# Moving the key and value weights, folding the query weights early, copying the first u spectrum on ScalarE, and re-routing the u loads in a fused attention and state-space kernel

## Chip, cores, metric

One core of one Trainium2 chip. The metric is device microseconds (us) of the whole kernel. Times quoted are medians; comparisons use ratios, explained with the result. A single core's run has no second die to compare with, so a run counts as slow only when it is over 1.5% above the fastest of the same kernel, and only fast runs are compared.

## The reference, cut to what matters

Two independent computations whose outputs are concatenated:

```python
# A: linear attention, x is 2048 x 448, 16 heads of 28
q, k, v = split(x @ wqkv)
pq, pk = q @ w_phi, k @ w_phi                       # per head
phi = concat([softmax(p), softmax(-p)])             # for pq and pk
kv, z = sum_s phi_k * v,  sum_s phi_k
a = (phi_q @ kv) / (phi_q @ z + 1e-6) @ wo
# B: state-space convolution, u is 2048 x 448, 256 states per channel
K[d, l] = real(sum_n C[d,n] * exp(dt[d] * A[d,n] * l) * dt[d] * B[d,n])
b = irfft(rfft(pad(u)) * rfft(pad(K))) + u * Dskip
```

## The kernel before

The kernel computes K as products of "low" tables W (49 small positions, by exponentials, sines and multiplies) and "high" tables U, multiplied on TensorE (`build_k`). It does the FFT as matmuls with a table G1; each half of u gives one "signal spectrum". The attention has a "key side" (16 tiles of x, accumulating KV) and a "query side". The weights w_phi are folded into the query and key weights (`fold_weights`) before use. All SBUF memory is one tile cut by hand at byte offsets; the framework finds the overlaps and sets the waits, and it chooses each engine's instruction order when it compiles, by rank and by its own estimate of time. At run time each engine follows that order: below, VectorE's state tables stand 4.16 us behind a sum of u that waits for its load.

The parts that the change touches:

```python
# memory (bytes per partition): W occupies oW .. oW+43904
Wqkv = sb("Wqkv", [112, 4, 3 * D_MODEL], BF16, oW)
wT = sb("wT", ..., oW + 10752); BD = sb("BD", ..., oW + 17920)
WpK = sb("WpK", [112, 4, D_MODEL], BF16, oW + 18816)      # folded key weights
# ... cut ...
def signal_spectrum(b, copy):
    ab = sb("ab", [128, 2, 4, D_MODEL], BF16, oVR)          # sums and differences of u
    for t in range(4):
        ua = sb("ua", [128, 2, D_MODEL], BF16, 0, bufs=2)   # two buffers, shared with the key side's EK
        for a in range(2):
            nc.gpsimd.dma_start(out=ua[64 * a:64 * a + 64, 0, :], in_=rep_rows(u2, 1024 * b, a, t))
        nc.gpsimd.dma_start(out=ua[:, 1, :], in_=pair_rows(u2, 1024 * b, t, 0))
        TT(out=ab[:, 0, t, :], in0=ua[:, 0, :], in1=ua[:, 1, :], op=ALU.add)
        TT(out=ab[:, 1, t, :], in0=ua[:, 0, :], in1=ua[:, 1, :], op=ALU.subtract)
    # ... cut: 8 x (two groups of 4 matmuls, each copied from PSUM by copy(); one store to SUd)
# ... cut: state tables, squarings, transposes of x ...
fold_weights(1, nc.vector.tensor_copy)                      # key weights
for _ in signal_spectrum(0, nc.vector.tensor_copy):         # first u spectrum
    pass

def key_side():                                             # 16 tiles
    for tt in range(16):
        pkv = ps_t.tile([128, 2, 512], F32, name="pkv", tag="arg", bufs=2)   # the tables' arguments use tag "arg" too
        # 4 matmuls with WpK, 4 with the value columns of Wqkv
        # ScalarE: two exponentials and a copy; VectorE: sums, reciprocal, multiply; TensorE: 8 accumulations
# ... cut ...
rotations(0)
with rank(9000):
    key_side()
with rank(8000):
    fold_weights(0, nc.scalar.copy)                         # query weights, after the key side
with rank(10000):
    for c in range(2):
        hi_tables(0, c)
more = signal_spectrum(1, nc.scalar.copy)                   # second u spectrum, interleaved with query_side
# for each quarter qt: dampings (low-table exponentials, ScalarE), damp (multiplies, VectorE), build_k
```

The softmax here doesn't subtract the row's maximum and nothing guards it: scores larger than these inputs give would overflow.

Of the kernel before, what the change touches and what calls it, by code (L numbers as in the profile page):

```python
# [10 lines left out]
BF16 = mybir.dt.bfloat16  # L11
# [6 lines left out]
D_MODEL = 448  # L18
# [70 lines left out]
def rep_rows(x2, row, a, t):  # L89
    rs = x2.ap[0][0]  # L90
    return bass.AP(tensor=x2.tensor, offset=x2[row + 256 * t + 128 * (1 - a), 0].offset,
                   ap=[[2 * rs, 64], [1, D_MODEL]])

def pair_rows(x2, row, t, col):
    rs = x2.ap[0][0]
    return bass.AP(tensor=x2.tensor, offset=x2[row + 1023 - 128 - 256 * t, col].offset,
                   ap=[[128 * rs, 2], [-2 * rs, 64], [1, D_MODEL]])
# [23 lines left out]
def kernel(  # L121
# [17 lines left out]
    nc = tc.nc  # L139
    out2 = out[0]  # L140
    x2 = A_x[0]
    u2 = B_u[0]
    TT = nc.vector.tensor_tensor
    act = nc.scalar.activation
    mm = nc.tensor.matmul
    consts = _dft_tables()
    G_d, GI_d, F_d, P_d, M_d = (nc.inline_tensor(t, name=f"const{i}").ap() for i, t in enumerate(consts))
# [4 lines left out]
    sb = Bytes(sb_pool.tile([128, 212800 // 2], BF16, name="sbuf"))  # L152
# [3 lines left out]
    oPID, oDSK, oMISC, oCB, oAT, oTH, oPW = 5376, 7424, 8320, 8960, 12544, 16128, 19712  # L156
    oW, oU, oT, oT2, oTs, oF, oSK0, oL = 44800, 88704, 117376, 138880, 146048, 151536, 158704, 173040
    PID = sb("PID", [128, 8, 128], BF16, oPID)
# [9 lines left out]
    xT = sb("xT", [112, 4, 2048], BF16, oF)  # L168
# [4 lines left out]
    KVZ = sb("KVZ", [112, 2, 4, 4, 2], BF16, o1 + 1792)  # L173
    HM = sb("HM", [112, 4, D_HEAD + 1], BF16, o1 + 1920)
    oSC, oRZ, oON, oOT, oOF, oVR, oZK, oV = (o1 + x for x in (2152, 3176, 4712, 8296, 10344, 12136, 15848, 16232))
    Wqkv = sb("Wqkv", [112, 4, 3 * D_MODEL], BF16, oW)
    wT = sb("wT", [112, 2, 4, D_MODEL], BF16, oW + 10752)
    BD = sb("BD", [112, 4, 112], BF16, oW + 17920)
    WpK = sb("WpK", [112, 4, D_MODEL], BF16, oW + 18816)

    ldt = sb("ldt", [112, 4], BF16, oMISC + 32)
    raw = {nm: sb(f"raw{nm}", [112, 4, SSM_N], BF16, oT + 2048 * i)
# [13 lines left out]
    for i in range(4):  # L196
        t = sb(f"xs{i}", [128, 4, D_MODEL], BF16, oW + 22400 + 3584 * i)
        nc.sync.dma_start(out=t[:, :, :], in_=x2[512 * i:512 * i + 512, :].rearrange("(t p) d -> p t d", p=128))
        XS.append(t)
    G1 = sb("G1", [128, 2, 4, 512], BF16, oG1)  # L200
    nc.sync.dma_start(out=G1[:, :, :, :], in_=G_d)
    nc.sync.dma_start(out=Wqkv[:, :, :], in_=A_wqkv.rearrange("(j p) n -> p j n", p=112))
    nc.gpsimd.memset(BD[:, :, :], 0.0)
    for hh in range(4):
        nc.gpsimd.dma_start(out=BD[28 * hh:28 * hh + 28, :, 28 * hh:28 * hh + 28],
                            in_=A_w_phi.rearrange("(c h) d f -> h d c f", h=4)[hh])
# [8 lines left out]
        return t.rearrange("p (g q x) -> p q g x", g=4, q=4)  # L215

    def signal_spectrum(b, copy):
        ab = sb("ab", [128, 2, 4, D_MODEL], BF16, oVR)
        for t in range(4):
            ua = sb("ua", [128, 2, D_MODEL], BF16, 0, bufs=2)  # L220
            for a in range(2):
                nc.gpsimd.dma_start(out=ua[64 * a:64 * a + 64, 0, :], in_=rep_rows(u2, 1024 * b, a, t))
            nc.gpsimd.dma_start(out=ua[:, 1, :], in_=pair_rows(u2, 1024 * b, t, 0))
            TT(out=ab[:, 0, t, :], in0=ua[:, 0, :], in1=ua[:, 1, :], op=ALU.add)  # L224
            TT(out=ab[:, 1, t, :], in0=ua[:, 0, :], in1=ua[:, 1, :], op=ALU.subtract)
        i = 0
        for st in range(2):
            for cp in range(2):
                for mp in range(2):
                    sg = sgs[i % 2]  # L230
                    i += 1
                    for k2 in range(2):
                        mt = 2 * mp + k2
                        p = mmt([128, 512])
                        for jt in range(4):
                            mm(p[:, 0:D_MODEL].rearrange("p (q g x) -> p q g x", q=4, g=4),  # L236
                               lhsT=G1[:, cp, jt, 128 * mt:128 * mt + 128], rhs=by_quarter(ab[:, cp ^ st, jt, :]),
                               start=(jt == 0), stop=(jt == 3))
                        copy(sg[:, k2, :], p[:, 0:D_MODEL])  # L239
                        if k2 == 0:  # L240
                            yield
                    nc.sync.dma_start(out=SUd[:, b, cp, st, 2 * mp:2 * mp + 2, :], in_=sg[:, :, :])
                    yield
# [58 lines left out]
    for half in range(2):  # L302
        hc, p = state_args(AT, half)
# [3 lines left out]
    for k in LOWP:  # L307
        for half in range(2):
            hc, p = state_args(TH, half)
# [22 lines left out]
    for tt in range(16):  # L332
        p = ps_t.tile([112, 4, 128], BF16, name="xp", tag="kb", bufs=2)
# [4 lines left out]
    def fold_weights(which, copy):  # L338
        for c in range(4):
            p = ps_t.tile([112, D_MODEL], BF16, name="wp", tag="kb", bufs=2)  # L340
            c0 = which * D_MODEL + 112 * c
            for j in range(4):
                nc.tensor.transpose(p[:, 112 * j:112 * j + 112], Wqkv[:, j, c0:c0 + 112], PID[0:112, 0, 0:112])
            copy(wT[:, which, c, :], p[:, :])
        for j in range(4):
            p = ps_t.tile([112, D_MODEL], F32, name="wp", tag="kb", bufs=2)
            for c in range(4):
                mm(p[:, 112 * c:112 * c + 112], lhsT=wT[:, which, c, 112 * j:112 * j + 112], rhs=BD[:, c, :],
                   start=True, stop=True)
            copy((WpQ, WpK)[which][:, j, :], p[:, :])  # L350

    fold_weights(1, nc.vector.tensor_copy)
    for _ in signal_spectrum(0, nc.vector.tensor_copy):
        pass
    V_ = [sb("V", [128, D_HEAD + 1, 16], BF16, oV, bufs=2) for _ in range(2)]
    for v in V_:
# [102 lines left out]
    def key_side():  # L459
        acc = [ps_t.tile([128, 512], F32, name="acc", tag="kb", bufs=2) for _ in range(2)]  # L460
        for tt in range(16):
            ts = slice(128 * tt, 128 * tt + 128)
            pkv = ps_t.tile([128, 2, 512], F32, name="pkv", tag="arg", bufs=2)
            for dj in range(4):
                mm(pkv[:, 0, 0:D_MODEL], lhsT=xT[:, dj, ts], rhs=WpK[:, dj, :], start=(dj == 0), stop=(dj == 3))
            for dj in range(4):
                mm(pkv[:, 1, 0:D_MODEL], lhsT=xT[:, dj, ts], rhs=Wqkv[:, dj, 2 * D_MODEL:], start=(dj == 0),
                   stop=(dj == 3))
            EK = sb("EK", [128, 2, D_MODEL], BF16, 0, bufs=2)
            for s in range(2):  # L470
                act(EK[:, s, :], pkv[:, 0, 0:D_MODEL], ACT.Exp, scale=1.0 - 2.0 * s)  # L471
            V = V_[tt % 2]
            nc.scalar.copy(V[:, 0:D_HEAD, :], pkv[:, 1, 0:D_MODEL].rearrange("p (h d) -> p d h", d=D_HEAD))
            zk = sb("zk", [128, 2, 16], F32, oZK, bufs=2)
            nc.vector.tensor_reduce(zk[:, :, :], EK[:, :, :].rearrange("p s (h f) -> p s h f", f=D_HEAD), axis=AX.X,  # L475
                                    op=ALU.add)
            rk = sb("rk", [128, 2, 16], BF16, oZK + 256, bufs=2)
            with nc.allow_low_precision(reason="bf16 softmax weights, as in the reference"):
                nc.vector.reciprocal(rk[:, :, :], zk[:, :, :])
            VR = sb("VR", [128, 2, D_HEAD + 1, 16], BF16, oVR, bufs=2)  # L480
            TT(out=VR[:, :, :, :], in0=V[:, :, :].unsqueeze(1).to_broadcast([128, 2, D_HEAD + 1, 16]),
               in1=rk[:, :, :].unsqueeze(2).to_broadcast([128, 2, D_HEAD + 1, 16]), op=ALU.mult)
            for s in range(2):
                for c in range(4):
                    mm(acc[s][0:112, 116 * c:116 * c + 116].rearrange("p (d h) -> p d h", h=4),  # L485
                       lhsT=EK[:, s, 112 * c:112 * c + 112], rhs=VR[:, s, :, 4 * c:4 * c + 4],
                       start=(tt == 0 and c == 0), stop=(tt == 15), skip_group_check=True)
        for s in range(2):
            a4 = acc[s][0:112, 0:464].rearrange("p (c d h) -> p c h d", c=4, h=4)
            TT(out=KVN[:, s], in0=a4[:, :, :, 0:D_HEAD],  # L490
               in1=HM[:, :, 0:D_HEAD].unsqueeze(1).to_broadcast([112, 4, 4, D_HEAD]), op=ALU.mult)
            TT(out=KVZ[:, s, :, :, 0], in0=a4[:, :, :, D_HEAD],
               in1=HM[:, :, 0].unsqueeze(1).to_broadcast([112, 4, 4]), op=ALU.mult)
            nc.vector.tensor_copy(KVZ[:, s, :, :, 1], HM[:, :, 0].unsqueeze(1).to_broadcast([112, 4, 4]))
# [183 lines left out]
    @contextmanager  # L678
    def rank(p):
        old = tc.cur_priority  # L680
        tc.cur_priority = p
        yield
        tc.cur_priority = old
# [4 lines left out]
    rotations(0)  # L688
    with rank(9000):
        key_side()  # L690
    with rank(8000):
        fold_weights(0, nc.scalar.copy)
    with rank(10000):
        for c in range(2):
            hi_tables(0, c)
# [89 lines left out]
```

## Time and profile before

| reading of the profiled run | before |
|---|---|
| median time (3 runs) | 390.0 us |
| VectorE / TensorE / ScalarE busy | 310.9 / 282.2 / 219.1 us |
| key side's last operation on VectorE ends | 114.5 us |
| first low-table exponential | 115.9 us |
| fourth tile of u's second half summed from | 128.1 us |
| large low-table multiplies start | 139.4 us |
| first build matmul | 157.0 us |
| activation table loads | 17 |

The table of windows, in four stretches: up to 50 us, to the end of the key side, to the first build matmul, to the end of the span. Columns: stretch, its length, then busy time and instruction count of each engine, the granted TensorE clock, the DMA share and GB/s.

```profile
core 0: us, PE busy (x) PEld busy (x) DVE busy (x) ACT busy (x) POOL busy (x), PEclk, DMA share, GB/s
0.00:50.00 50.00, 20.70 (x138) 14.47 (x139) 33.42 (x40) 32.21 (x50) 11.19 (x23) 0.88 0.64 159
50.00:114.50 64.50, 54.04 (x382) 32.48 (x381) 60.44 (x127) 28.43 (x59) 4.58 (x11) 0.96 0.11 35
114.50:157.00 42.50, 28.56 (x184) 16.30 (x184) 22.42 (x49) 24.36 (x45) 5.43 (x9) 0.72 0.16 47
157.00:390.00 233.00, 178.93 (x3078) 140.93 (x3076) 194.65 (x335) 134.09 (x230) 12.93 (x17) 0.85 0.29 83
```

In the second stretch VectorE is the fullest (60.4 of 64.5 us). In the third no engine is full: that is the hole.

What ScalarE does at the edge of the hole, from its timeline (start, duration, engine, line, operation, operands, and in brackets the idle time before it and what ended it). L471 and L473 are the key side, L344 a copy of the query fold, L407 a low-table exponential:

```profile
109.91 0.54 ACT L473 CAST sbuf<-pkv 128x448 bf16<-128x448 f32 x1
114.41 1.58 ACT L344 COPY sbuf<-wp 112x448 bf16<-112x448 bf16 x3 [3.96 <-PE wp L343]
115.88 0.93 ACT L407 ACTIVATE sbuf<-arg 128x896 bf16<-128x896 f32 x1
116.69 0.55 ACT L344 COPY sbuf<-wp 112x448 bf16<-112x448 bf16 x1
```

ScalarE stands idle for 4 us, then the fold goes first. Further on, in ScalarE's queue a query exponential (L504) waits for the query projection on TensorE (L501):

```profile
120.39 1.01 ACT L407 ACTIVATE sbuf<-arg 128x896 bf16<-128x896 f32 x1
127.61 1.08 ACT L504 ACTIVATE sbuf<-mmt 112x512 bf16<-112x512 f32 x2 [6.21 <-PE mmt L501]
128.58 0.55 ACT L407 ACTIVATE sbuf<-arg 128x448 bf16<-128x448 f32 x1
```

That projection in turn stands in TensorE's queue behind the second spectrum (L236), which waits for the third tile of u:

```profile
126.62 0.53 PE L236 MATMUL mmt<-sbuf 128*128 128x448 bf16 x1 [4.59 <-DVE sbuf L224]
```

TensorE had finished the tables' arguments by 111.4 us, and the fold was over at 120.6. On VectorE inside the hole (L224 is a sum of u, L419 a low-table multiply):

```profile
118.77 0.39 DVE L224 TENSOR_TENSOR sbuf<-sbuf 128x448 bf16<-128x448 bf16 x1 [4.25 <-DMA sbuf<-in_B_u_dram]
...
126.17 0.39 DVE L224 TENSOR_TENSOR sbuf<-sbuf 128x448 bf16<-128x448 bf16 x1 [4.86 <-DMA sbuf<-in_B_u_dram]
...
128.09 0.39 DVE L224 TENSOR_TENSOR sbuf<-sbuf 128x448 bf16<-128x448 bf16 x1
...
135.75 0.60 DVE L419 TENSOR_TENSOR sbuf<-sbuf 128x112 bf16<-128x112 bf16 x4 [6.97 <-ACT sbuf L404]
...
139.40 0.97 DVE L419 TENSOR_TENSOR sbuf<-sbuf 128x1680 bf16<-128x1680 bf16 x1
```

And the start of VectorE's timeline (L336 copies a transposed tile of x; L254 is the first state-table multiply, which everything else in the state tables follows):

```profile
10.43 0.42 DVE L336 COPY sbuf<-xp 112x512 bf16<-112x512 bf16 x1 [9.57 <-PE xp L335]
15.02 0.39 DVE L224 TENSOR_TENSOR sbuf<-sbuf 128x448 bf16<-128x448 bf16 x1 [4.16 <-DMA sbuf<-in_B_u_dram]
15.33 0.16 DVE L247 TENSOR_SCALAR sbuf<-sbuf 112x4 bf16<-112x4 bf16 x1
15.40 2.36 DVE L254 TENSOR_TENSOR sbuf<-sbuf 112x1024 f32<-112x1024 bf16 x2
```

VectorE's queue stands 4.16 us at the first sum of u, for a load, with the state tables behind it.

### The profile page before, as it was taken

Reading aid. Unit: us, or ns where it says so; the run is one execution under the profiler, and the core shown is the slowest. Engines: PE = TensorE matmul, PEld = TensorE weight load, DVE = VectorE, ACT = ScalarE, POOL = GpSimd, SP = SyncE. Lnnn points to the kernel's source line nnn. Section 1 sums busy time; section 2 is a strip of 40 time slices with the busy share of each in tenths; the row PEclk is TensorE's granted clock in tenths of the full one; section 3 lists DMA queues with packets and bytes.
Section 4 is the critical chain, followed back from the end, with each engine's and each line's share of the span. In section 5 each row is a group of like instructions: output and inputs, shape, how many; then the busy total and the mean of one; then the engine's idle time right before and its main releaser. Section 6 shows DMA issues by size and latency. Waiting matters only on the chain.

```text
span 389.2 us, 9018 instructions
## 1 busy us (share of the span) xinstructions
PE 282.2 (73%) x3780; PEld 204.2 (52%) x3780; DVE 310.9 (80%) x548; ACT 219.1 (56%) x381; POOL 34.1 (9%) x59
## 2 busy tenths in 40 slices
PE   0294478988863859996787799677970596956994
PEld 0261353455452335674554576445860485945994
DVE  0598988999961279996459988998996979999872
ACT  1289972055554764799985846942949323212431
POOL 7100220000033000000000000001000000054000
PEclk9999569999995687999659699885986888796999
DMA  7990212200012001213000100120922218397005
GB/s 184 284 254 28 63 28 72 94 24 2 0 30 64 28 25 45 70 56 96 26 24 25 25 28 26 24 79 24 278 97 56 52 52 290 104 205 180 14 3 189
DMA packets 31105, 31.60 MB, mean 81 GB/s; under 512 B 11560, under 2 KB 28680, under 8 KB 30680
## 3 DMA queue, kind: packets, MB, share of 16 engines
q1 hardware_dynamic: 24216, 22.65, 20.1%
q0 software_dynamic: 4064, 7.23, 7.2%
q10 hardware_dynamic: 2784, 1.15, 1.3%
q8 instruction: 29, 0.48, 0.5%
q14 instruction: 12, 0.10, 0.1%
HBM read 23.07 MB, written 7.34 MB: 78 GB/s over the span
## 4 chain that ended last, share of the span: by engine, by line
PE 37%; DVE 20%; ACT 17%; DMA 11%; issue 7%; SPq 4%; POOL 3%; DVEq 0%; POOLq 0%; ACTq 0%
PE kb L453 10%; PE mmt L593 6%; DMA sbuf<-in_B_u_dram 5%; PE mmt L545 4%; PE mmt L236 3%; PE yo L634 3%; SPq L567 3%; ACT sbuf L504 3%; DVE sbuf L475 3%; DMA sbuf<-SUd 3%; PE mmt L501 3%; PE arg L373 2%; PE mmt L539 2%; DMA sbuf<-const 2%; DVE sbuf L239 2%
## 5 line engine op out<-in xcount | busy, mean ns | idle before, releaser
L453 PE MATMUL kb<-sbuf 128*16 128x49 bf16 x1792 | 49.3, 274 | 3.7 <-issue 2.9
L593 PE MATMUL mmt<-sbuf 128*128 128x112 bf16 (+1 forms) x336 | 34.4, 272 | 22.2 <-ACT sbuf L596 9.7
L419 DVE TENSOR_TENSOR sbuf<-sbuf 128x112 bf16<-128x112 bf16 (+1 forms) x64 | 37.4, 619 | 13.2 <-ACT sbuf L404 12.8
L453 PEld LDWEIGHTS <-sbuf 128*16 128x16 bf16 x1792 | 41.5, 118 | 9.4 <-issue 7.8
L236 PE MATMUL mmt<-sbuf 128*128 128x448 bf16 x128 | 34.0, 390 | 14.2 <-DVE sbuf L224 6.5
L593 PEld LDWEIGHTS <-sbuf 128*128 128x128 bf16 x336 | 28.6, 118 | 28.5 <-issue 11.2
L425 DVE TENSOR_TENSOR sbuf<-sbuf 128x896 bf16<-128x896 bf16 (+1 forms) x48 | 35.6, 775 | 0.2
L596 ACT CAST sbuf<-mmt 128x448 bf16<-128x448 f32 x32 | 16.2, 549 | 27.1 <-PE mmt L593 27.1
L634 PE MATMUL yo<-sbuf 128*128 128x112 bf16 (+1 forms) x384 | 28.8, 228 | 2.9 <-DMA sbuf<-const 1.8
L471 ACT ACTIVATE sbuf<-pkv 128x448 bf16<-128x448 f32 x32 | 15.8, 552 | 26.5 <-PE acc L485 19.1
L532 DVE TENSOR_TENSOR sbuf<-mmt,sbuf 128x448 bf16<-128x448 f32 x32 | 19.4, 622 | 11.0 <-PE mmt L529 10.7
L634 PEld LDWEIGHTS <-sbuf 128*128 128x128 bf16 x384 | 26.1, 98 | 3.5 <-DMA sbuf<-const 2.0
L610 DVE TENSOR_TENSOR sbuf<-sbuf 128x1792 bf16<-128x1792 bf16 (+1 forms) x18 | 24.4, 1400 | 3.5 <-ACT sbuf L596 3.3
L407 ACT ACTIVATE sbuf<-arg 128x896 bf16<-128x896 f32 (+1 forms) x32 | 25.8, 874 | 1.4 <-PE kb L453 1.4
L236 PEld LDWEIGHTS <-sbuf 128*128 128x128 bf16 x128 | 13.1, 106 | 19.9 <-issue 11.5
L641 ACT CAST sbuf<-yo 128x224 bf16<-128x224 f32 (+1 forms) x24 | 9.0, 410 | 25.2 <-PE yo L636 25.2
L373 PE MATMUL arg<-sbuf 128*128 128x224 bf16 x128 | 22.0, 320 | 1.3 <-ACT sbuf L404 0.7
L504 ACT ACTIVATE sbuf<-mmt 112x512 bf16<-112x512 f32 x32 | 17.2, 601 | 9.8 <-PE mmt L501 9.6
L545 PE MATMUL mmt<-sbuf 112*128 112x448 bf16 x64 | 19.6, 436 | 3.6 <-ACT sbuf L541 3.5
L501 PE MATMUL mmt<-sbuf 112*112 112x512 bf16 x64 | 19.4, 426 | 1.9 <-ACT sbuf L504 1.9
L286 DVE TENSOR_TENSOR sbuf<-sbuf 128x1792 bf16<-128x1792 bf16 (+3 forms) x33 | 20.1, 609 | 0.7
L287 DVE TENSOR_TENSOR sbuf<-sbuf 128x1792 bf16<-128x1792 bf16 (+3 forms) x33 | 19.8, 603 | 0.0
(117 smaller groups left out, 590.5 us busy)
## 6 DMA issues: line engine op xcount, KB each, us to landing
sbuf<-const SPq DMA_DIRECT2D x32, 224.0 KB
SUd<-sbuf SPq DMA_DIRECT2D x16, 224.0 KB
sbuf<-const SPq DMA_DIRECT2D x2, 1024.0 KB
sbuf<-in_A_x_dram SPq DMA_DIRECT2D x4, 448.0 KB
out_dram<-sbuf SPq DMA_DIRECT2D x16, 112.0 KB
sbuf<-SUd POOLq DMA_DIRECT2D x1, 1792.0 KB, 12.6
sbuf<-in_B_u_dram SPq DMA_DIRECT2D x4, 448.0 KB
sbuf<-SUd POOLq DMA_DIRECT2D x2, 896.0 KB, 9.2
```

The costliest lines, as they stand in the source:

```text
L236: mm(p[:, 0:D_MODEL].rearrange("p (q g x) -> p q g x", q=4, g=4), lhsT=G1[:, cp, jt, 128 * mt:128 * mt + 128], rhs=by_quarter(ab[:, cp ^ s ...
L373: mm(p[:, e // 2, (e % 2) * QC:(e % 2 + 1) * QC], lhsT=PID[:, 4 * grp + e, :], rhs=src[:, part, cols], start=(part == 0), stop=(part == 1))
L407: act(dst.rearrange("p c (a b) x -> p a b c x", b=2), src.rearrange("p a b (c x) -> p a b c x", c=2), ACT.Exp, scale=float(sgn * f))
L419: TT(out=W[:, c, cs_, r, :], in0=W[:, c, cs_ if sgn < 0 else 0, r, :], in1=T[:, cs_, j0:j0 + n, xs], op=ALU.mult)
L425: TT(out=(t2[:, :, 0:n, :], dst)[1 - i], in0=src, in1=PW[512][:, i, cols].unsqueeze(1).unsqueeze(1).to_broadcast([128, 2, n, COLS]), op=AL ...
L453: mm(p[32 * g:32 * g + N_HI, qq * N_LO:(qq + 1) * N_LO], lhsT=U[qt % 2][c][:, :, ri, xc], rhs=W[:, c, ri, :, xc], start=(i == 0), stop=(i ...
L501: mm(p[:, :], lhsT=WpQ[:, dj, 112 * c:112 * c + 112], rhs=xT[:, dj, 512 * sc:512 * sc + 512], start=(dj == 0), stop=(dj == 3))
L504: act(EQ[:, s, c, :], p[:, :], ACT.Exp, scale=1.0 - 2.0 * s)
L545: mm(pf[:, :], lhsT=oT_[:, c, :], rhs=wo[:, c, :], start=(c == 0), stop=(c == 3))
L593: mm(p[:, k2, :].rearrange("p (q g x) -> p q g x", q=nq, g=4), lhsT=f_tiles[i][1][:, fi, :], rhs=natural(Kt[:, kt, :], gi), start=(n == 0) ...
L610: TT(out=t[:, :, :], in0=su, in1=sk, op=ALU.mult)
L634: mm(p[:, k2, :], lhsT=GI[r][:, cp, mt, 128 * jt:128 * jt + 128], rhs=S[:, r, cp, mt, :], start=(cp == 0 and mt == 0), stop=False)
```

## The change

Its intent: let the low tables start before the key side is done, by moving the key and value weights out of W's memory and folding the query weights early; relieve VectorE of the first spectrum's copies; bring u by the sync queue.

```diff
-    Wqkv = sb("Wqkv", [112, 4, 3 * D_MODEL], BF16, oW)
-    wT = sb("wT", [112, 2, 4, D_MODEL], BF16, oW + 10752)
-    BD = sb("BD", [112, 4, 112], BF16, oW + 17920)
-    WpK = sb("WpK", [112, 4, D_MODEL], BF16, oW + 18816)
+    Wqk = sb("Wqk", [112, 4, 2 * D_MODEL], BF16, oW)
+    wT = sb("wT", [112, 2, 4, D_MODEL], BF16, oW + 7168)
+    BD = sb("BD", [112, 4, 112], BF16, oW + 14336)
+    WpK = sb("WpK", [112, 4, D_MODEL], BF16, oPW + 17920)
+    WV = sb("WV", [112, 4, D_MODEL], BF16, oPW + 21504)
     # ... cut: Wqk and WV loaded right after x, the G1 load moved behind the folds
     def signal_spectrum(b, copy):
-        ab = sb("ab", [128, 2, 4, D_MODEL], BF16, oVR)
+        ab = sb("ab", [128, 2, 4, D_MODEL], BF16, oT + 14336)
         for t in range(4):
-            ua = sb("ua", [128, 2, D_MODEL], BF16, 0, bufs=2)
+            ua = sb(f"ua{b}", [128, 2, D_MODEL], BF16, (oON, 0)[b], bufs=(4, 2)[b])
     # ... cut: the three loads into ua by nc.sync instead of nc.gpsimd
     fold_weights(1, nc.vector.tensor_copy)
-    for _ in signal_spectrum(0, nc.vector.tensor_copy):
+    fold_weights(0, nc.scalar.copy)
+    nc.sync.dma_start(out=G1[:, :, :, :], in_=G_d)
+    for _ in signal_spectrum(0, nc.scalar.copy):
         pass
     # ... cut: the value matmuls read WV
     with rank(9000):
         key_side()
-    with rank(8000):
-        fold_weights(0, nc.scalar.copy)
```

More of the change, by code (lines that the diff above doesn't have):

```diff
@@ L199 @@
         XS.append(t)
+    wq3 = A_wqkv.rearrange("(j p) n -> p j n", p=112)
+    nc.sync.dma_start(out=Wqk[:, :, :], in_=wq3[:, :, 0:2 * D_MODEL])
+    nc.sync.dma_start(out=WV[:, :, :], in_=wq3[:, :, 2 * D_MODEL:])
     G1 = sb("G1", [128, 2, 4, 512], BF16, oG1)
-    nc.sync.dma_start(out=G1[:, :, :, :], in_=G_d)
-    nc.sync.dma_start(out=Wqkv[:, :, :], in_=A_wqkv.rearrange("(j p) n -> p j n", p=112))
     nc.gpsimd.memset(BD[:, :, :], 0.0)
@@ L217, in signal_spectrum @@
     def signal_spectrum(b, copy):
-        ab = sb("ab", [128, 2, 4, D_MODEL], BF16, oVR)
+        ab = sb("ab", [128, 2, 4, D_MODEL], BF16, oT + 14336)
         for t in range(4):
-            ua = sb("ua", [128, 2, D_MODEL], BF16, 0, bufs=2)
+            ua = sb(f"ua{b}", [128, 2, D_MODEL], BF16, (oON, 0)[b], bufs=(4, 2)[b])
             for a in range(2):
-                nc.gpsimd.dma_start(out=ua[64 * a:64 * a + 64, 0, :], in_=rep_rows(u2, 1024 * b, a, t))
-            nc.gpsimd.dma_start(out=ua[:, 1, :], in_=pair_rows(u2, 1024 * b, t, 0))
+                nc.sync.dma_start(out=ua[64 * a:64 * a + 64, 0, :], in_=rep_rows(u2, 1024 * b, a, t))
+            nc.sync.dma_start(out=ua[:, 1, :], in_=pair_rows(u2, 1024 * b, t, 0))
             TT(out=ab[:, 0, t, :], in0=ua[:, 0, :], in1=ua[:, 1, :], op=ALU.add)
@@ L342, in fold_weights @@
             for j in range(4):
-                nc.tensor.transpose(p[:, 112 * j:112 * j + 112], Wqkv[:, j, c0:c0 + 112], PID[0:112, 0, 0:112])
+                nc.tensor.transpose(p[:, 112 * j:112 * j + 112], Wqk[:, j, c0:c0 + 112], PID[0:112, 0, 0:112])
             copy(wT[:, which, c, :], p[:, :])
@@ L466, in key_side @@
             for dj in range(4):
-                mm(pkv[:, 1, 0:D_MODEL], lhsT=xT[:, dj, ts], rhs=Wqkv[:, dj, 2 * D_MODEL:], start=(dj == 0),
+                mm(pkv[:, 1, 0:D_MODEL], lhsT=xT[:, dj, ts], rhs=WV[:, dj, :], start=(dj == 0),
                    stop=(dj == 3))
```

## The prediction

> **What bounds it now.** VectorE is fullest (the page's busy times): 310.9 us of 389.2; TensorE 282.2, ScalarE 219.1. The table of windows shows three stretches:
>
> - 20 to 114 us: VectorE 84 to 100% busy; in 77 to 114 it has 35.4 of 37 us. TensorE is not far behind (30.4).
> - 114 to 139 us: a hole. VectorE works 5.3 of 25 us, TensorE 16.7 at a granted clock of 0.66, ScalarE 16.8. By the timeline the key side ends at 114.4 us; then the query weights are folded (to 120.6), the first low-table exponential runs at 115.9, the second half of u lands by GpSimd at 118.8, 120.6, 126.2 and 128.1, and the query projection waits on TensorE behind the second spectrum (4.6 us for the third u tile). The large low-table multiplies start only at 139.4.
> - After 139 us: no such hole except 190 to 207 (VectorE 8.5 of 17 us); 160 to 190 is ScalarE's (29.5 of 30).
>
> **What the change does.**
>
> 1. The 16 copies of the first u spectrum (9.25 us of VectorE, windows of that line) go to ScalarE, which has 2.9 of 17 us busy in 60 to 77. They shared a VectorE-bound stretch with the key side. I credit 7 us, since TensorE has about 50 us of matmuls from 57 us on (0.19 us per 448 columns). Key side ends at about 107.
> 2. The query fold moves from 114–121 us to about 52–60, where ScalarE idles: 4.1 us of ScalarE off the hole, and the query projection can start early.
> 3. The low tables wait for the key side only through two PSUM buffers, shared with their arguments, which came free at 109 to 110.5 us while the first exponential ran at 115.9: about 5 us.
> 4. u goes by the sync queue. Landing took a median 4.1 and 5.3 us by GpSimd; the Trainium skill, "DMA: Bandwidth & Descriptors" (Specifications), gives the hardware path the lower first-byte latency, 0.6 against 1 us. No run here shows it yet for u. The tiles still wait for the key side's exponential buffers, two at a time. I expect the fourth 8 us after the key side instead of 14.
>
> No arithmetic is added. The first sums of u now wait for squaring scratch until about 48 us, but were complete only at 59 before.
>
> **On the critical path.** Large low-table multiplies before: 139.4 us, 25 after the key side. After: key side 107, then eight exponentials and the negations (6.9 + 3.7 us of ScalarE) shared with query exponentials: about 116. Gain there about 23 us. Later stages have the same work and shift; I take off 1 to 2 us for the ScalarE stretch, which gets denser, and a lower clock.
>
> Predicted: 367 us, range 355 to 379. Faster by over 2%: 0.92; within 2%: 0.06; slower: 0.02.
>
> **What would show each step.** (1) VectorE total 302 us; key side's last multiply at 105–109. (2) Fold copies before 62 us. (3) First low-table exponential within 3 us of the last key-side one. (4) u landing in 2–4 us, fourth tile by 116. (5) Hole under 8 us of VectorE idle; the span from first build matmul (157.0 us before) to the end unchanged within 4 us.
>
> **What would make it wrong.** TensorE limiting the key side, so that step 1 gives nothing; in-order queues tying exponentials or u loads behind something later; the gain eaten at 160–207 us by ScalarE, with more activation table loads (ten between 159 and 190 now).

## The result

367.3 us (median of 4 runs, 365.5 to 368.4) against 390.1 us. Ratio 0.9402, 95% interval 0.9351 to 0.9453. A ratio here is the mean time of one kernel's fast runs over that of the other's fast runs of the same rounds, so it is not quite the ratio of the medians. In a second session on another chip the same kernel measured 0.9447 (0.9414 to 0.9480); that value is the yardstick for the experiments.

| reading of the profiled run | before | after |
|---|---|---|
| span | 389.2 us | 365.3 us |
| VectorE / TensorE / ScalarE busy | 310.9 / 282.2 / 219.1 | 305.1 / 276.7 / 216.2 |
| transposes to states start | 17.75 | 13.37 |
| query fold, last copy ends | 120.6 | 58.5 |
| key side's last operation on VectorE ends | 114.5 | 105.2 |
| first low-table exponential | 115.9 | 101.9 |
| fourth tile of u's second half summed from | 128.1 | 117.9 |
| large low-table multiplies start | 139.4 | 112.7 |
| first build matmul | 157.0 | 135.5 |
| first build matmul to the end | 232.2 | 229.8 |
| activation table loads | 17 | 9 |

The windows of after, cut at the same events (the first cut, at 50 us, is a time and not an event, so the earlier start shows as a shorter second stretch):

```profile
core 0: us, PE busy (x) PEld busy (x) DVE busy (x) ACT busy (x) POOL busy (x), PEclk, DMA share, GB/s
0.00:50.00 50.00, 24.69 (x168) 17.49 (x168) 37.10 (x51) 36.55 (x58) 5.88 (x18) 0.78 0.54 145
50.00:105.00 55.00, 51.85 (x386) 31.02 (x385) 51.54 (x100) 39.76 (x81) 0.04 (x1) 0.98 0.18 58
105.00:135.00 30.00, 19.08 (x104) 10.24 (x104) 20.48 (x45) 13.75 (x26) 0.00 (x0) 0.66 0.18 58
135.00:366.00 231.00, 181.03 (x3126) 139.77 (x3124) 195.96 (x338) 126.19 (x228) 12.86 (x17) 0.88 0.29 84
```

The second stretch shrank by 9.5 us and the third by 12.5; the last stayed. In the second, TensorE (51.9 of 55) and VectorE (51.5) are now equally full. The third still has a hole: from 105.2 to 126.3 us VectorE works 11.8 of 21.1 us.

ScalarE at the edge (L477 is the key side, L508 a query exponential, L411 a low-table exponential):

```profile
100.44 0.54 ACT L477 CAST sbuf<-pkv 128x448 bf16<-128x448 f32 x1
100.85 1.11 ACT L508 ACTIVATE sbuf<-mmt 112x512 bf16<-112x512 f32 x2
101.92 4.22 ACT L411 ACTIVATE sbuf<-arg 128x896 bf16<-128x896 f32 x6
```

The low tables follow the key side without a pause, and now six of them run in a row before the next query exponential. VectorE in the hole (L226 is a sum of u, L423 a low-table multiply):

```profile
110.68 0.39 DVE L226 TENSOR_TENSOR sbuf<-sbuf 128x448 bf16<-128x448 bf16 x1 [2.18 <-DMA sbuf<-in_B_u_dram]
...
112.69 1.03 DVE L423 TENSOR_TENSOR sbuf<-sbuf 128x1680 bf16<-128x1680 bf16 x1 [0.80 <-ACT sbuf L411]
115.10 0.39 DVE L226 TENSOR_TENSOR sbuf<-sbuf 128x448 bf16<-128x448 bf16 x1 [1.38 <-DMA sbuf<-in_B_u_dram]
...
117.91 0.39 DVE L226 TENSOR_TENSOR sbuf<-sbuf 128x448 bf16<-128x448 bf16 x1 [1.17 <-DMA sbuf<-in_B_u_dram]
```

u is still what VectorE waits for. The chain of waits of after (start, length, what) names it twice, and the lengths are about that of the one in the chain of before (5.25 us at 120.8):

```profile
104.73 5.83 DMA sbuf<-in_B_u_dram
...
112.58 5.21 DMA sbuf<-in_B_u_dram
```

And the start: the state tables no longer stand behind a sum of u, L256 being the same multiply as L254 of before:

```profile
10.19 0.85 DVE L338 COPY sbuf<-xp 112x512 bf16<-112x512 bf16 x2 [2.64 <-PE xp L337]
10.96 0.16 DVE L249 TENSOR_SCALAR sbuf<-sbuf 112x4 bf16<-112x4 bf16 x1
11.02 2.35 DVE L256 TENSOR_TENSOR sbuf<-sbuf 112x1024 f32<-112x1024 bf16 x2
```

### The profile page after: what moved, and what is told of

The parts are those of the page before. It is cut to its first block, busy times and chain, and to the rows that moved or that the text cites. A ratio compares the mean times of both kernels' runs of the same rounds, so it can differ in the third digit from the quotient of the medians.

```text
span 365.3 us, 8990 instructions
## 1 busy us (share of the span) xinstructions
PE 276.7 (76%) x3780; PEld 198.5 (54%) x3780; DVE 305.1 (84%) x532; ACT 216.2 (59%) x389; POOL 18.8 (5%) x35
## 4 chain that ended last, share of the span: by engine, by line
PE 39%; DVE 27%; ACT 14%; DMA 13%; issue 4%; SPq 2%; DVEq 0%; ACTq 0%
PE kb L457 12%; DMA sbuf<-const 5%; PE mmt L597 5%; PE mmt L238 4%; DVE sbuf L479 4%; PE mmt L549 4%; PE yo L638 3%; PE mmt L505 3%; DMA sbuf<-in_B_u_dram 3%; DVE sbuf L423 3%; DVE sbuf L485 3%; DMA sbuf<-sbuf 3%; ACT sbuf L411 3%; DMA sbuf<-in_A_x_dram 2%; PE mmt L543 2%
## 5 line engine op out<-in xcount | busy, mean ns | idle before, releaser
L457 PE MATMUL kb<-sbuf 128*16 128x49 bf16 x1792 | 51.3, 274 | 4.1 <-issue 3.3
L597 PE MATMUL mmt<-sbuf 128*128 128x112 bf16 (+1 forms) x336 | 33.0, 261 | 21.4 <-ACT sbuf L600 10.0
L597 PEld LDWEIGHTS <-sbuf 128*128 128x128 bf16 x336 | 26.8, 111 | 27.9 <-issue 11.4
L423 DVE TENSOR_TENSOR sbuf<-sbuf 128x112 bf16<-128x112 bf16 (+1 forms) x64 | 36.9, 618 | 5.8 <-ACT sbuf L408 4.7
L600 ACT CAST sbuf<-mmt 128x448 bf16<-128x448 f32 x32 | 16.3, 548 | 25.2 <-PE mmt L597 25.2
L638 PEld LDWEIGHTS <-sbuf 128*128 128x128 bf16 x384 | 26.2, 98 | 3.2 <-DMA sbuf<-const 1.7
L241 ACT CAST sbuf<-mmt 128x448 bf16<-128x448 f32 x32 | 17.3, 548 | 15.7 <-issue 7.2
L411 ACT ACTIVATE sbuf<-arg 128x896 bf16<-128x896 f32 (+1 forms) x32 | 24.8, 863 | 1.5 <-PE kb L457 1.1
L508 ACT ACTIVATE sbuf<-mmt 112x512 bf16<-112x512 f32 x32 | 17.2, 600 | 10.5 <-PE mmt L505 10.3
L238 PEld LDWEIGHTS <-sbuf 128*128 128x128 bf16 x128 | 12.6, 104 | 17.8 <-issue 9.4
L549 PE MATMUL mmt<-sbuf 112*128 112x448 bf16 x64 | 18.2, 409 | 4.9 <-ACT sbuf L545 4.9
L288 DVE TENSOR_TENSOR sbuf<-sbuf 128x1792 bf16<-128x1792 bf16 (+3 forms) x33 | 20.1, 610 | 0.8
L377 PE MATMUL arg<-sbuf 128*128 128x224 bf16 x128 | 20.4, 300 | 0.6 <-ACT sbuf L408 0.5
```

What stands on the lines that cost most here:

```text
L238: mm(p[:, 0:D_MODEL].rearrange("p (q g x) -> p q g x", q=4, g=4), lhsT=G1[:, cp, jt, 128 * mt:128 * mt + 128], rhs=by_quarter(ab[:, cp ^ s ...
L288: TT(out=tmp, in0=src, in1=pw(1), op=ALU.mult)
L377: mm(p[:, e // 2, (e % 2) * QC:(e % 2 + 1) * QC], lhsT=PID[:, 4 * grp + e, :], rhs=src[:, part, cols], start=(part == 0), stop=(part == 1))
L411: act(dst.rearrange("p c (a b) x -> p a b c x", b=2), src.rearrange("p a b (c x) -> p a b c x", c=2), ACT.Exp, scale=float(sgn * f))
L423: TT(out=W[:, c, cs_, r, :], in0=W[:, c, cs_ if sgn < 0 else 0, r, :], in1=T[:, cs_, j0:j0 + n, xs], op=ALU.mult)
L457: mm(p[32 * g:32 * g + N_HI, qq * N_LO:(qq + 1) * N_LO], lhsT=U[qt % 2][c][:, :, ri, xc], rhs=W[:, c, ri, :, xc], start=(i == 0), stop=(i ...
```

## The experiments

The total came out as predicted, so the question was whether it did for the reasons given. The traces already cast doubt on two: u did not land sooner, and the start gained 4.4 us that the prediction doesn't mention. Each experiment ran in 5 rounds beside the kernel before; all outputs were correct. "x us" behind a difference of ratios is that difference times 390 us.

### after_again: the yardstick

The changed kernel, unedited.

> The changed kernel itself, as the yardstick for the runs beside it: 366 to 368 us, 0.938 to 0.944 of the kernel before.

Measured: 369.3 us, 0.9447 (0.9414 to 0.9480). That is just above the range I named and 0.5% above the first session. Runs of different sessions are therefore compared to no better than half a per cent.

### a_memory_back: is the memory move worth anything?

```diff
-    WpK = sb("WpK", [112, 4, D_MODEL], BF16, oPW + 17920)
-    WV = sb("WV", [112, 4, D_MODEL], BF16, oPW + 21504)
+    WpK = sb("WpK", [112, 4, D_MODEL], BF16, oW + 15232)
+    WV = sb("WV", [112, 4, D_MODEL], BF16, oW + 18816)
```

> The changed kernel with key and value weights put back into the low tables' memory (everything else kept; the instruction order of TensorE, VectorE and ScalarE is the same). Theory A: the low tables are held by the two PSUM buffers they share with the key side, which come free at the same moment as these weights, so the move is worth nothing by itself: within 2 us of the changed kernel, first low-table exponential still at 101 to 103 us. It also lets four filter tiles load before 25 us instead of at 98, beside the u loads, so it may be 0 to 2 us faster. Rival B (the change's title): the memory is what held the tables: 3 to 8 us slower, first low-table exponential 3 us or more later.

Measured: 369.1 us, 0.9449 (0.9425 to 0.9473), the same as the changed kernel in the same session. ScalarE's timeline at the edge:

```profile
100.55 0.54 ACT L477 CAST sbuf<-pkv 128x448 bf16<-128x448 f32 x1
100.96 1.11 ACT L508 ACTIVATE sbuf<-mmt 112x512 bf16<-112x512 f32 x2
102.04 1.73 ACT L411 ACTIVATE sbuf<-arg 128x896 bf16<-128x896 f32 x2
```

The first low-table exponential follows the key side as before the edit, 1.5 us after the last key copy starts. So the move that names the change is worth nothing that these runs can see. Why it is worth nothing is argued and not tested by an edit. The last reader of those weights is the key side's last projection (L471); in this trace it ends at 99.7 us, 2.4 us before the first low-table exponential, so the memory is free in time. The tables' arguments need the PSUM buffers of those same projections and stand behind them on TensorE, and on ScalarE a query exponential runs until 102.07: any of these comes later than the release of the memory.

### b_fold_early: the fold alone, weights still in W's memory

```diff
     fold_weights(1, nc.vector.tensor_copy)
+    fold_weights(0, nc.scalar.copy)
...
-    with rank(8000):
-        fold_weights(0, nc.scalar.copy)
```

> The kernel before with the query fold done early by ScalarE, nothing else. Theory A: it takes the fold out of the hole and with it what held the low tables (the query weights shared their memory and were read last by the fold): 378 to 384 us, first low-table exponential within 3 us of the last key-side one. Rival B: without the memory move the tables still wait, and the u loads by GpSimd set the hole's length: 387 to 390 us.

Measured: 381.2 us, 0.9798 (0.9759 to 0.9836), a gain of 7.9 us. In its trace:

```profile
109.79 0.54 ACT L474 CAST sbuf<-pkv 128x448 bf16<-128x448 f32 x1
110.20 4.25 ACT L408 ACTIVATE sbuf<-arg 128x896 bf16<-128x896 f32 x6
```

The tables start right after the key side although all weights still lie in W. What held the first of them by about 5 us was the fold: it ran after the key side (its transposes waited for VectorE to empty the key side's accumulators, whose PSUM buffers it shares, 1.8 us in four waits), it stood before the tables in ScalarE's queue, and it read weights out of W's memory. Which of these ties was the tighter is not told apart, as the edit takes away all of them.

The 5 us are the smaller part. The edit also changed the compiled order: all eight of the larger low-table exponentials are now done by 117.1 us, ahead of the first query exponential at the edge (121.5), and no longer behind the one that waits for u. The large low-table multiplies start at 121.0 us instead of 139.4, although u lands as late as before (its fourth tile is summed from 127.9, before from 128.1). The first build matmul comes at 145.3 instead of 157.0.

Activation table loads fell from 17 to 9: the compiled order no longer mixes query exponentials with sines in the stretch up to 200 us. I had feared the opposite. That the fewer loads belong to the gain is not shown: from the first build matmul to the end it takes 232.4 us against 232.2 (with 45 more matmuls in it), and a_u_early below has 13 loads and is faster than the changed kernel with 9.

### b_copies_act and a_copies_dve: the first spectrum's copies

```diff
-    for _ in signal_spectrum(0, nc.vector.tensor_copy):
+    for _ in signal_spectrum(0, nc.scalar.copy):
```

This line alone, on the kernel before:

> The kernel before with the first u spectrum copied by ScalarE, nothing else. Theory A: the key side is VectorE's and ends 5 to 9 us earlier, and the end with it: 381 to 385 us. Rival B: TensorE limits the key side as soon as VectorE is relieved: key side ends at most 3 us earlier, 387 to 390 us.

Measured: 386.6 us, 0.9933 (0.9895 to 0.9972): 2.6 us, between the two theories. The key side does end 4.3 us earlier (110.2), and the first build matmul comes 4.5 us earlier (152.5), so the old hole passes the lead on whole. What is lost is lost after it: from the first build matmul to the end these profiles have 233.4 us against 232.2.

The line taken back, in the changed kernel:

> The changed kernel with the first u spectrum copied by VectorE again. Theory A (VectorE sets the key side): 4 to 9 us slower than the changed kernel, 371 to 376 us. Rival B (TensorE sets it: 9.7 of 10 us busy from 60 to 100): 0 to 3 us slower, 367 to 370 us.

Measured: 372.7 us, 0.9555 (0.9519 to 0.9591), 4.2 us slower than the yardstick (of another session, so give or take some 2 us). From 50 us to about the end of its key side, which comes at 107.9 us against 104.8 in the yardstick:

```profile
50.00:107.70 57.70, 51.32 (x384) 30.97 (x385) 56.62 (x115) 33.18 (x69) 0.00 (x0) 1.00 0.15 51
```

VectorE works 56.6 of 57.7 us here, against 51.5 of 55 with ScalarE copying. So VectorE did set the key side, and relieving it of 9.25 us bought about 4; that it bought no more fits TensorE, with some 51 us of work, being the next limit. The first build matmul is no milestone here: it comes at 134.8 us, before the yardstick's 136.3, with more of the query's work left for after it.

### b_fold_copies: fold and copies together

The two edits above, on the kernel before.

> The kernel before with two things of the change: query fold early by ScalarE, and the first u spectrum copied by ScalarE. Alone they gave 8 us and 2.6 us. Theory A: they add up, with about 4 us for the copies as seen when they were undone in the changed kernel: 375 to 380 us, the rest of the way to 368 being the start and u's buffers. Rival B: they overlap, 380 to 383 us, and the start and u's buffers are worth over 11 us together.

Measured: 374.6 us, 0.9600 (0.9556 to 0.9644), just below theory A's range, a gain of 15.6 us: more than 7.9 + 2.6. On top of the early fold the copies are worth 7.7 us (across two sessions, so give or take some 2 us). So neither single-edit figure is "the" value of that part. Perhaps one edit alone leaves a wait that the other would have ended; no run isolates it.

### b_ab_moved and b_ab_ua4: the start that was not predicted

First only the place of the sums of u, on the kernel before:

```diff
-        ab = sb("ab", [128, 2, 4, D_MODEL], BF16, oVR)
+        ab = sb("ab", [128, 2, 4, D_MODEL], BF16, oT + 14336)
```

> The kernel before with one thing of the change: the sums of u go to the squaring scratch. Theory A: VectorE's in-order queue stood at the first sum of u from 10.9 to 15.0 us, waiting for u, and the tables behind it; with the sums elsewhere that sum comes after 47 us and the start runs 4.4 us earlier: 384 to 387 us, transposes to states start near 13.4 us, not 17.75. Rival B: the 4 us are given back at the key side (VectorE bound by the same work) or the wait was for another load: 389 to 391 us.

Measured: 390.5 us, 1.0006 (0.9949 to 1.0063): nothing, to within about 2 us. The start does run earlier (transposes to states at 13.1 us), but at the end of the key side only 1.7 us of it are left (112.8). VectorE's timeline shows where the rest is given back:

```profile
55.04 0.39 DVE L224 TENSOR_TENSOR sbuf<-sbuf 128x448 bf16<-128x448 bf16 x1 [0.35 <-DMA sbuf<-in_B_u_dram]
55.35 0.38 DVE L225 TENSOR_TENSOR sbuf<-sbuf 128x448 bf16<-128x448 bf16 x1
58.04 0.39 DVE L224 TENSOR_TENSOR sbuf<-sbuf 128x448 bf16<-128x448 bf16 x1 [2.31 <-DMA sbuf<-in_B_u_dram]
```

The last sum of the first half comes at 58.0 us (58.9 before), because u has two buffers and the last two tiles can't be fetched until the first two are summed. So I gave the first half its four buffers as well:

```diff
-            ua = sb("ua", [128, 2, D_MODEL], BF16, 0, bufs=2)
+            ua = sb(f"ua{b}", [128, 2, D_MODEL], BF16, (oON, 0)[b], bufs=(4, 2)[b])
```

> The kernel before with the sums of u in the squaring scratch and the first half of u in four buffers of its own (still by GpSimd). Theory A: with two buffers the early start was lost again at 55 to 59 us, where VectorE waited for the last u tile; with four they lie ready, and the 4 us reach the key side: key side's last multiply at 109 to 111 us, 384 to 388 us in all. Rival B: the key side is VectorE's and TensorE's work and in-order queues give the start back in any case: 388 to 391 us.

Measured: 386.2 us, 0.9878 (0.9837 to 0.9920), a gain of 4.8 us. In its timeline the last two sums of the first half follow without a wait:

```profile
56.70 0.38 DVE L224 TENSOR_TENSOR sbuf<-sbuf 128x448 bf16<-128x448 bf16 x1
57.00 0.38 DVE L225 TENSOR_TENSOR sbuf<-sbuf 128x448 bf16<-128x448 bf16 x1
```

The key side ends at 110.1 us instead of 114.5, and the first build matmul comes at 151.9 instead of 157.0. (This profile caught the slowest of the six runs, 389.6 us at a granted clock of 0.826, so its later stages are not compared.) The two edits together carry the start's gain through; the first alone does not.

### a_u2_gpsimd: the queue of the u loads

In the changed kernel the second half of u is fetched by GpSimd again:

```diff
-                nc.sync.dma_start(out=ua[64 * a:64 * a + 64, 0, :], ...)
-            nc.sync.dma_start(out=ua[:, 1, :], ...)
+                (nc.sync, nc.gpsimd)[b].dma_start(out=ua[64 * a:64 * a + 64, 0, :], ...)
+            (nc.sync, nc.gpsimd)[b].dma_start(out=ua[:, 1, :], ...)
```

> The changed kernel with the second half of u fetched by GpSimd's queue again (same buffers; VectorE's and ScalarE's order is the same). Theory A (this study's reading of the traces): the sync queue is not the quicker one for these loads; the whole-tile load took 5.2 to 5.8 us from issue to use there against a median 5.3 us by GpSimd, so the move of the queue gave nothing at this place: within 2 us of the changed kernel. Rival B (the prediction's step 4): the sync queue is quicker and this costs 3 to 6 us.

Measured: 369.6 us, 0.9469 (0.9434 to 0.9503), against 0.9447 for the sync queue in another session: no difference beyond the noise. The load that the fourth tile waits for is issued at 112.90 us and the sum follows 5.5 us later, at 118.4; in the profile of the changed kernel it is issued at 112.58 and the sum follows 5.3 us later, at 117.9. The load in the chain of waits of a_u2_gpsimd, to set beside the 5.83 and 5.21 us above:

```profile
112.90 5.34 DMA sbuf<-in_B_u_dram
```

This agrees with the Trainium skill, "DMA: Bandwidth & Descriptors" (Issuing engines are not separate DMA queues): the transfers run on the same 16 engines whoever issues them, and another issuer saves only issue time.

### a_u_early, a_mem_u_early, a_best: what is left of the hole

The second half of u gets the four buffers of the first half, so it is no longer tied to the key side's exponential buffers:

```diff
-            ua = sb(f"ua{b}", [128, 2, D_MODEL], BF16, (oON, 0)[b], bufs=(4, 2)[b])
+            ua = sb("ua", [128, 2, D_MODEL], BF16, oON, bufs=4)
```

> The changed kernel with the second half of u in the four buffers the first half used, so that it loads and is summed before the key side ends. Theory A: what is left of the hole is u's landing (5.2 to 5.8 us twice on the chain of waits, TensorE idle 7.4 us before the second spectrum between 103 and 119 us): 359 to 363 us, first build matmul 5 to 8 us earlier than 135.5. Rival B: the hole is ScalarE's table exponentials and negations (until 116): at most 2 us gained, 365 to 367 us.

Measured: 361.9 us, 0.9278 (0.9242 to 0.9314), 6.6 us faster than the changed kernel. The time is theory A's, its milestone is not: the first build matmul comes at 139.1 us, later than 136.3 in the yardstick. The key side, now interleaved with u's second half, ends at 109.7. What was gained lies after it: the query's first reciprocal comes at 111.5 us instead of 125.7, so the second spectrum's and first query block's work no longer runs beside the build. From the first build matmul to the end it takes 220.4 us instead of 228.2 (at a granted clock of 0.86 there against 0.87, so it is not the clock).

With the weights also back in W's memory (both edits together):

> Both of the edits above together. Theory A: like u early alone, within 2 us, as the filter tiles' loads then collide with nothing that waits. Rival B: 3 to 8 us slower than u early alone, as the memory holds the tables.

Measured: 360.1 us, 0.9200 (0.9163 to 0.9237; one of its six runs was slow and doesn't count). This is the fastest version: 2.6% below the changed kernel of the same session (0.9200 over 0.9447). It is 0.8% under u early alone, with the two intervals just apart. It keeps W's old memory plan, so the "freed" memory may even have cost something here. In the kernel before, four filter tiles were loaded in advance (from 14.25 us) into the memory that the change gives to the weights; with the weights there, those four loads are issued from 97.8 us, in the busy stretch. That they are the cause of the 0.8% was not isolated, and there is a rival: four of the five fast runs had a granted clock of 0.894 to 0.897, against 0.866 to 0.885 in u early alone, and the fifth, at 0.875, took 361.4 us, about the time of u early alone (361.9).

Last, the second half's loads by GpSimd's idle queue, in that version:

> The changed kernel with the weights back in the tables' memory and the second half of u early in four buffers, now fetched by GpSimd's idle queue rather than the sync queue. The instruction order of TensorE, VectorE and ScalarE is that of the run with both edits (0.920 of before). Theory A: there the sync queue, in order, held the first spectrum's stores behind u loads that waited for VectorE (56 to 59 us), which delayed the first key exponential from 63.1 to 66.3 us; that goes, 2 to 4 us faster: 0.910 to 0.916. Rival B: the delay is the order of the instructions, no gain: 0.918 to 0.923.

Measured: 361.0 us, 0.9209 (0.9163 to 0.9254): no gain, so theory A falls. In a_mem_u_early ScalarE's spectrum copies wait for stores to SUd:

```profile
60.87 0.97 ACT L241 CAST sbuf<-mmt 128x448 bf16<-128x448 f32 x2 [1.95 <-DMA SUd<-sbuf]
...
64.02 0.97 ACT L241 CAST sbuf<-mmt 128x448 bf16<-128x448 f32 x2 [2.19 <-DMA SUd<-sbuf]
```

In a_best, with nothing else in the sync queue there, they still do:

```profile
62.73 0.97 ACT L241 CAST sbuf<-mmt 128x448 bf16<-128x448 f32 x2 [3.33 <-DMA SUd<-sbuf]
```

So it was not the sync queue's order that held the stores. In both versions loads of u are in flight beside them, and in the changed kernel, where they are not, the same wait is 0.46 us. That the loads slow the stores fits this, but no run isolates it.

## Why the prediction was right

The total (367 forecast, 367.3 measured) and the direction were right, and so was the main step: with the fold and the copies moved, the low tables follow the key side, and the hole shrinks. Term by term the exact hit was partly luck:

1. **Copies off VectorE: direction right, size too large.** I credited 7 us. Undoing it in the changed kernel costs 4.2 us; alone it gives 2.6, on top of the early fold 7.7. The reason given for less than 9.25 (TensorE next in line) is what the windows show: 51.9 of 55 us busy. The key side ended at 105.2, inside the 105 to 109 named; of the 9.3 us, the copies alone give 4.3 (b_copies_act) and the start with u's buffers 4.4 (b_ab_ua4). VectorE's total is 305.1 us, not the 302 named.
2. **Query fold early: right.** Its copies end at 58.5 us (62 named). Alone it gives 7.9 us. I had credited "4.1 us of ScalarE" and, for the tables, "about 5 us"; what the fold's move mostly did I had not named: it put the low-table exponentials ahead of a query exponential that waited for u.
3. **The low tables' wait: event right, cause wrong.** The first low-table exponential comes 1.5 us after the last key-side copy starts (3 named). But I listed it as an effect of the change, that is, of the key and value weights leaving W; putting them back changes nothing (0.9449 against 0.9447). The late fold, and the order that was compiled with it, were the holder (b_fold_early).
4. **u by the sync queue: failed.** I named landing in 2 to 4 us and the fourth tile 8 us after the key side, by 116 us. Measured: 5.2 to 5.8 us on the chain, the fourth tile at 117.9, which is 12.7 us after the key side (13.6 before). The Trainium skill's 0.6 against 1 us of first-byte latency ("DMA: Bandwidth & Descriptors", Specifications) is a difference of 0.4 us in a load that takes over 5; it could not have carried the 6 us that I put on it, and a_u2_gpsimd shows no gain.
5. **The missing term: the start.** VectorE's 4.16 us at the head of its queue at 10.9 us was in the trace, and the diff moved both the sums that caused it and the buffers that would have given it back. b_ab_ua4 measures it, with the buffers, at 4.8 us. In the prediction the move of the sums appears only as a possible cost.
6. **The hole: nearly.** VectorE idles 9.3 us in it (under 8 named). The large low-table multiplies came at 112.7 us, earlier than the 116 of the sum, a gain of 26.7 us; 21.5 of these were left at the first build matmul. By the totals of waits between 100 and 130 us, u's tiles account for 4.7 us of VectorE's waiting and, behind those sums, 7.5 us of TensorE's. With u early TensorE fills the place (33.5 of 39 us busy from 100 to 139, against 19.1 of 30 from 105 to 135 in the changed kernel), while VectorE still idles 8.9 us in those 39; so u explains TensorE's part of the hole and not the whole of VectorE's. The rest of the run, from first build matmul to the end, stayed within 4 us as named (229.8 against 232.2), and the feared extra activation table loads became fewer: 9 for 17. Each takes 1.28 us in the trace, the figure for the load itself of the Trainium skill, "ScalarE: Activation LUTs" (What ACT_TABLE_LOAD costs).

So there were over-estimates (the copies, and u's queue by about 5 us for the fourth tile) and an omission (the start, about 4.5 us) that happened to cancel; that they do so us by us is not shown. As a check of the sum: fold and copies together 15.6 us, start and buffers 4.8 us, the second half's queue and the memory 0, which makes 20.4 us of the 21.6 (0.9447) to 23.3 (0.9402) measured. It is a rough check, as the fold and the copies did not add up either. The earlier load of the weights, the later load of G1 and the sync queue for the first half of u were not tested alone.

## What to carry to other kernels

Before crediting a memory move, look for what else holds the same stage: here the memory was free 2.4 us before it was needed, and the actual holder was a small fold placed behind the long stage, with a compiled order that let one late load of u hold the tables through two queues. Follow such a chain from queue to queue, and not only to the first wait. Read the first microseconds of each engine's in-order queue: one early instruction that waits for a load delays everything behind it, and removing that wait pays only if the buffers downstream can keep the lead. When a load is late, give it buffers that free early before changing the queue that issues it; and when a prediction's total comes out right, test its terms all the same.

## What the Trainium skill lacked or had wrong

- "DMA: Bandwidth & Descriptors" (Issuing engine by pattern) calls the sync path generally faster. For these loads of 112 KB, in rows of 896 bytes, no advantage was seen: 5.2 to 5.8 us from issue to landing on the chain of waits by the sync queue, a median 5.3 us in the listing of the kernel before and 5.6 in that of a_u2_gpsimd by GpSimd, and 0.9447 against 0.9469 for the whole kernel.
- The same page (Anatomy of one DMA) fits a GpSimd-issued load as 2.0 us plus bytes over 436e3 per us; for 112 KB that would be an estimate of 2.3 us. The listing of DMA issues of the kernel before has a median of 5.3 us from issue to landing for eight such loads. The page gives no figure for several partial loads into one tile in flight together, as here.
- No page says how to tell which of several ties holds a stage, when an SBUF overlap, a PSUM buffer pair and the order of the queues all could: here the SBUF overlap was worth 0.0% (0.9449 against 0.9447), while the fold's place in the order was worth 7.9 us.
